# Loading q for two chunks at a time, and transposing q and k by the DMA from chunk 8 on, in a retention kernel fused with a feed-forward

## The chip, the cores and the metric

The kernel runs on one core of a Trainium2 chip. The core has five engines with instruction streams of their own: TensorE (PE; its weight loads are listed apart as PEld), VectorE (DVE), ScalarE (ACT), GpSimd (POOL) and SyncE (SP), which here issues the DMAs. The metric is the device time of one execution in microseconds, as the median of several runs. Profiles come from one execution with the hardware profiler on.

## The reference

Per batch and head a recurrent state is decayed and read at each token; the result, with the heads side by side, goes through a feed-forward with a product in the middle.

```python
batch, n_heads, seq, head_dim = (4, 8, 768, 64)
gamma = 1.0 - 2.0 ** (-5.0 - np.arange(H, dtype=np.float32))
for t in range(S):
    state = gamma[None, :, None, None] * state + np.einsum('bhd,bhe->bhde', k[:, :, t], v[:, :, t])
    y[:, :, t] = scale * np.einsum('bhd,bhde->bhe', q[:, :, t], state)
...
x = np.ascontiguousarray(attn_out.transpose(0, 2, 1, 3)).reshape(B * S, H * D)
a = x @ w1
b = x @ w2
h = a * b @ w3
return (h @ w_out).astype(np.float32)
```

All inputs and the output are float32; x is 3072 x 512, w1 and w2 are 512 x 1024, w3 is 1024 x 1024 and w_out 1024 x 512.

## The kernel before

The sequence is cut into chunks of 128 tokens, six for each of the four batches, 24 in all. Heads go in four pairs p, so that one pair fills 128 partitions. Work is done in float16 with float32 sums. The order of all instructions is written out by hand: each engine takes its own in the order of the Python code, and semaphores join them.

At the start w3 and w_out are multiplied into one matrix W3O (w3_transpose, w3_mm), while weights and the first chunks are loaded; chunks 0 and 1 and the feed-forward's first block are woven into this. From chunk 2 on, step(n) does one chunk:

- load_chunk(n+4) issues the loads of q, k and v of a later chunk on the SP queue (L61), each 128 tokens by 8 heads of 64 floats.
- casts(n+2) on GpSimd makes q16 and k16 (L214, L216) and the scaled v in vp (L220).
- transposes(n+1) on TensorE turns the four 128x128 blocks of k16 and the four of q16 through the identity into one PSUM tile psT (L234, L236). ScalarE copies k into kp (L239, L240): head 0 of a pair on the upper 64 partitions, head 1 on the lower, zeros elsewhere, so that one matmul works on one head. VectorE copies q into qT (L241).
- scores(n): eight matmuls of kp with qT (L252, psA), masked by VectorE into am (L255).
- kv(n): the chunk's contribution to the state (L273, psK); VectorE adds the old state (L281), GpSimd multiplies by the decay (L282). In a batch's last chunk kv does nothing.
- outputs(n): vp with am, and the old state with qT, summed in psY (L290, L291, L293); VectorE scales it into XT (L294), the transposed x.

Between these parts fill.pull puts in units of the feed-forward for blocks of 256 tokens: an a unit and a b unit (four matmuls each, L310; ScalarE copies a into pa, L320; VectorE multiplies into ht, L326), and o units (eight matmuls, L331; ScalarE scales into osb, L336; SP stores it, L338). fill is a queue; each pull takes a quarter of the units that the finished tokens allow in this step. What is left after the last step is run at the end.

XT is one tile for all tokens. The pools give q16 two buffers and k16 three; each chunk tensor loaded has six.

Of the kernel before, what the change touches and what calls it, by code (L numbers as in the profile page):

```python
# [9 lines left out]
FP = mybir.dt.float32  # L10
HP = mybir.dt.float16
AF = mybir.ActivationFunctionType
MULT = mybir.AluOpType.mult
# [5 lines left out]
def kernel(  # L19
# [15 lines left out]
    NCH = S // C  # L35
    NSTEP = B * NCH
    NTOK = B * S
    NP = H // 2
    DM = 512
    DFF = 1024  # L40
# [7 lines left out]
    xpool = ctx.enter_context(tc.tile_pool(name="xpool", bufs=1))  # L48
# [11 lines left out]
    def dma_in(dst, src):  # L60
        nc.sync.dma_start(dst, src)  # L61

    chunk_in = {}

    def load_chunk(n):
        if n >= NSTEP:
            return
        b, c = divmod(n, NCH)
        tiles = []
        for nm, src in (("q", q), ("k", k), ("v", v)):  # L70
# [51 lines left out]
    nc.gpsimd.iota(if_i[:, :], pattern=[[1, 128]], base=1, channel_multiplier=0)  # L122
    LGH = const.tile([128, H], FP, name="LGH")
    LGP = const.tile([128, NP], FP, name="LGP")
    for h in range(H):
# [5 lines left out]
    nc.gpsimd.memset(keep[:, :], 1.0)  # L131
    nc.gpsimd.affine_select(
        out=keep[:, :], in_=keep[:, :], compare_op=mybir.AluOpType.is_ge, fill=0.0,
        base=0, pattern=[[1, 128]], channel_multiplier=-1,
    )


# [16 lines left out]
        nc.vector.memset(GS[r : r + 64, p, r : r + 64], gam[h] ** C)  # L154
    zero(VP[2])

    XT = xpool.tile([128, NP, NTOK], HP, name="xt")

# [47 lines left out]
    q16s, k16s, qTs, ATs = {}, {}, {}, {}  # L206
    Tst = [None]

    def casts(n):
        if n >= NSTEP:  # L210
            return
        q32, k32, v32 = chunk_in.pop(n)
        q16 = att.tile([128, 512], HP, tag="q16", name="q16")
        nc.gpsimd.tensor_copy(q16[:, :], q32[:, :])  # L214
        k16 = att.tile([128, 512], HP, tag="k16", name="k16", bufs=3)
        nc.gpsimd.tensor_copy(k16[:, :], k32[:, :])  # L216
        vp = VP[n % 3]

        for r in range(2):
            nc.gpsimd.tensor_tensor(  # L220
                vp[:, :, r, r * 64 : r * 64 + 64],
                v32[:, :].rearrange("j (p s e) -> j p s e", s=2, e=64)[:, :, r, :],
                VS[:, :].rearrange("j (p s) -> j p s", s=2)[:, :, r].unsqueeze(2).broadcast_to((128, NP, 64)),
                MULT,
            )
        q16s[n], k16s[n] = q16, k16

    def transposes(n):
        if n >= NSTEP:
            return  # L230
        q16, k16 = q16s.pop(n), k16s[n]
        ps = ps_t.tile([128, 2, NP, 128], HP, tag="psT", name="psT")
        for p in range(NP):
            nc.tensor.transpose(ps[:, 1, p, :], k16[:, p * 128 : (p + 1) * 128], ident16[:, :])  # L234
        for p in range(NP):
            nc.tensor.transpose(ps[:, 0, p, :], q16[:, p * 128 : (p + 1) * 128], ident16[:, :])  # L236
        kp = KP[n % 2]
        qT = att.tile([128, NP, 128], HP, tag="qT", name="qT")
        nc.scalar.copy(kp[0:64, :, 0, :], ps[0:64, 1, :, :])  # L239
        nc.scalar.copy(kp[64:128, :, 1, :], ps[64:128, 1, :, :])  # L240
        nc.vector.tensor_copy(qT[:, :, :], ps[:, 0, :, :])  # L241
        qTs[n] = qT

    def scores(n):
        qT, kp = qTs[n], KP[n % 2]
        am = att.tile([128, NP, 2, 128], HP, tag="am", name="am")
        for half in range(2):
            ps = ps_at.tile([128, 2, 2, 128], FP, tag=f"psA{half}", name=f"psA{half}")
            for i in range(2):
                p = half * 2 + i  # L250
                for r in range(2):
                    nc.tensor.matmul(  # L252
                        ps[:, i, r, :], lhsT=kp[:, p, r, :], rhs=qT[:, p, :], start=True, stop=True
                    )
            nc.vector.tensor_tensor(  # L255
                am[:, half * 2 : half * 2 + 2, :, :].rearrange("j p s i -> j (p s) i"),
                ps[:, :, :, :].rearrange("j p s i -> j (p s) i"),
                keep[:, :].unsqueeze(1).broadcast_to((128, 4, 128)),
                MULT,
            )  # L260
        ATs[n] = am

    def kv(n):
        k16, vp = k16s.pop(n), VP[n % 3]
        c = n % NCH
        if c == NCH - 1:
            return None
        ps = ps_at.tile([128, NP, 128], FP, tag="psK", name="psK")
        for p in range(NP):

            rhs = vp[:, p, :, :].rearrange("j s e -> j (s e)")
            rhs = bass.AP(rhs.tensor, rhs.offset, [list(rhs.ap[0]), [192, 2], [1, 64]])
            nc.tensor.matmul(  # L273
                ps[:, p, :], lhsT=k16[:, p * 128 : (p + 1) * 128], rhs=rhs, start=True, stop=True
            )
        t16 = att.tile([128, NP, 128], HP, tag="t16", name="t16")
        if c == 0:
            nc.vector.tensor_tensor(t16[:, :, :], ps[:, :, :], GS[:, :, :], MULT)
        else:
            s32 = att.tile([128, NP, 128], FP, tag="s32", name="s32")  # L280
            nc.vector.tensor_tensor(s32[:, :, :], ps[:, :, :], Tst[0][:, :, :], ADD)  # L281
            nc.gpsimd.tensor_tensor(t16[:, :, :], s32[:, :, :], GS[:, :, :], MULT)  # L282
        return t16

    def outputs(n, t_new):
        am, qT, vp = ATs.pop(n), qTs.pop(n), VP[n % 3]
        c = n % NCH
        ps = ps_at.tile([128, NP, 128], FP, tag="psY", name="psY")
        for p in range(NP):
            nc.tensor.matmul(ps[:, p, :], lhsT=vp[:, p, 0, :], rhs=am[:, p, 0, :], start=True, stop=False)  # L290
            nc.tensor.matmul(ps[:, p, :], lhsT=vp[:, p, 1, :], rhs=am[:, p, 1, :], start=False, stop=(c == 0))  # L291
            if c > 0:
                nc.tensor.matmul(ps[:, p, :], lhsT=Tst[0][:, p, :], rhs=qT[:, p, :], start=False, stop=True)  # L293
        nc.vector.tensor_tensor(  # L294
            XT[:, :, n * C : (n + 1) * C], ps[:, :, :], YS[:, :, :], MULT
        )
        Tst[0] = t_new

# [3 lines left out]
    class Ffn:  # L302
# [4 lines left out]
        def mm(self, W, f):  # L307
            ps = ps_f.tile([128, TB], FP, tag="psF", name="psF")
            for d in range(4):
                nc.tensor.matmul(  # L310
                    ps[:, :], lhsT=W[d][:, f * 128 : (f + 1) * 128],
                    rhs=XT[:, d, self.tok0 : self.tok0 + TB],
                    start=(d == 0), stop=(d == 3),
                )
            return ps
# [62 lines left out]
    def step(n):  # L378

        ready = n * C  # L380
        share = fill.available(ready) / (2 - n % 2)
        casts(n + 2)
        transposes(n + 1)
        fill.pull(share * 0.25, ready)
        scores(n)
        fill.pull(share * 0.25, ready)
        t_new = kv(n)
        fill.pull(share * 0.25, ready)
        outputs(n, t_new)
        fill.pull(share * 0.25, ready)  # L390

    def cast_w(W, st, d, on_dve):
# [26 lines left out]
    w3_transpose(4)  # L419
    casts(0)  # L420
    w3_mm(3)
    transposes(0)
    cast_w3(5)
    w3_mm(4)
# [34 lines left out]
    def by_rows(W, ps, d):  # L459
        for f in range(8):  # L460
            nc.tensor.matmul(
                ps[f // 2][:, f % 2, :], lhsT=W[d][:, f * 128 : (f + 1) * 128],
                rhs=XT[:, d, 0:TB], start=(d == 0 and f % 2 == 0),
                stop=(d == 3 and f % 2 == 1),
            )

# [10 lines left out]
    for d in range(4):  # L477
        by_rows(W2, ps, d)
        if d == 1:
            transposes(2)  # L480
            casts(3)
    for i in range(4):
# [45 lines left out]
```

## Time and profile before

| | |
|---|---|
| median of 3 runs | 209.92 us (209.89 to 210.04) |
| profiled execution | 210.8 us |
| its span, first to last instruction | 209.0 us |
| granted TensorE clock | 1.000 |
| DMA: packets, bytes | 81239, 35.96 MB |
| of the packets, under 512 bytes | 75584 |

The span is what the profile shows; the profiled execution's own time is 1.8 us longer, and 0.9 us above the median. In the page's slices each digit is the busy share of a fortieth of the span in tenths. Groups give busy time in all, the mean of one in nanoseconds and the idle time before. Matmuls are pipelined, so the time of one in a group is longer than what it adds to a stream; the chain of work shows the latter. In rows of windows stand the stretch and its length, the busy time of PE, PEld, DVE, ACT and POOL with the number of instructions, the granted clock, the DMA share and GB/s.

### The profile page before, as it was taken

To read this page: it belongs to the slowest core of one execution; us is meant where nothing else is said; L and a number is where in the kernel's file an instruction comes from. 1 tells how busy PE (TensorE), PEld (TensorE's weight loads), DVE (VectorE), ACT (ScalarE), POOL (GpSimd) and SP (SyncE) were. 2 spreads that over 40 slices of the span, in tenths; PEclk is the share of its full clock that TensorE was granted. 3 is DMA by queue.
4 is the path that set the end of the run, shared out by engine and by line. 5 is a ranking of instruction groups with operands and counts; after the bars stand their busy time and mean duration, and the time that the engine had idled before them with its cause. 6 is when DMAs were issued, how large, how long until landed. Compare 5 with 4: busy or idle time off the path is not lost.

```text
span 209.0 us, 4850 instructions
## 1 busy us (share of the span) xinstructions
PE 197.2 (94%) x1848; PEld 148.3 (71%) x1848; DVE 118.6 (57%) x243; ACT 91.3 (44%) x187; POOL 78.5 (38%) x138
## 2 busy tenths in 40 slices
PE   6979699889999999999999999999999999999992
PEld 1435476666899778777877787787778877877750
DVE  4553479457777476448545854684367447753310
ACT  6463694343554425532544354335424542533331
POOL 4005302276895343663533336536331462010000
PEclk9999999999999999999999999999999999999999
DMA  6999999999999888459756865795578110111112
GB/s 231 390 359 211 305 391 413 216 221 207 232 252 207 185 168 188 109 117 195 162 116 129 201 157 111 139 201 139 115 153 200 57 49 4 50 50 53 50 50 102
DMA packets 81239, 35.96 MB, mean 172 GB/s; under 512 B 75584, under 2 KB 75584, under 8 KB 81216
## 3 DMA queue, kind: packets, MB, share of 16 engines
q1 hardware_dynamic: 81216, 35.66, 67.9%
q8 instruction: 14, 0.23, 0.5%
q14 instruction: 9, 0.07, 0.1%
HBM read 29.36 MB, written 6.29 MB: 171 GB/s over the span
## 4 chain that ended last, share of the span: by engine, by line
PE 76%; DMA 11%; SPq 6%; ACT 2%; DVE 2%; issue 1%; POOL 0%; ACTq 0%
PE psF L310 38%; PE psO L331 18%; DMA stg<-in_moe_w_dram 8%; SPq L61 6%; PE psA L252 4%; PE psW L199 2%; PE psT L234 2%; PE psT L236 2%; PE psY L290 2%; DMA k<-in_k_dram 2%; PE psY L291 2%; PE psY L293 2%; PE psK L273 2%; DVE am L255 1%; ACT kp L239 1%
## 5 line engine op out<-in xcount | busy, mean ns | idle before, releaser
L310 PE MATMUL psF<-xt,w 128*128 128x256 f16 x704 | 87.5, 272 | 0.2
L310 PEld LDWEIGHTS <-w 128*128 128x128 f16 x704 | 67.0, 97 | 9.6 <-issue 0.9
L320 ACT COPY pa<-psF 128x256 f32<-128x256 f32 x88 | 31.1, 373 | 36.3 <-PE psF L310 35.9
L331 PE MATMUL psO<-w3o,ht 128*128 128x512 f16 x192 | 45.0, 379 | 0.0
L282 POOL TENSOR_TENSOR t<-s,GS 128x512 f16<-128x512 f32 x16 | 20.3, 1270 | 58.3 <-DVE s L281 58.3
L241 DVE COPY qT<-psT 128x512 f16<-128x512 f16 x24 | 10.2, 425 | 55.7 <-ACT kp L240 55.7
L326 DVE TENSOR_TENSOR ht<-pa,psF 128x256 f16<-128x256 f32 x88 | 35.1, 416 | 10.6 <-ACT pa L320 6.1
L336 ACT ACTIVATE osb<-psO 128x512 f32<-128x512 f32 x24 | 14.3, 597 | 51.6 <-PE psO L331 51.6
L220 POOL TENSOR_TENSOR vp<-v,VS 128x256 f16<-128x256 f32 x48 | 28.5, 615 | 11.9 <-PE psY L291 6.9
L255 DVE TENSOR_TENSOR am<-psA,keep 128x512 f16<-128x512 f32 x48 | 30.8, 683 | 0.7 <-PE psA L252 0.7
L331 PEld LDWEIGHTS <-ht 128*128 128x128 f16 x192 | 17.9, 98 | 17.5
L214 POOL CAST q<-q 128x512 f16<-128x512 f32 x24 | 14.6, 610 | 23.2 <-DMA q<-in_q_dram 20.8
L216 POOL CAST k<-k 128x512 f16<-128x512 f32 x24 | 14.7, 614 | 10.5 <-PE psK L273 5.4
L294 DVE TENSOR_TENSOR xt<-psY,YS 128x512 f16<-128x512 f32 x24 | 16.6, 690 | 1.7 <-PE psY L293 0.5
L239 ACT COPY kp<-psT 64x512 f16<-64x512 f16 x24 | 13.7, 571 | 8.2 <-PE psT L236 8.2
L290 PE MATMUL psY<-am,vp 128*128 128x128 f16 x96 | 16.7, 219 | 0.2
L291 PE MATMUL psY<-am,vp 128*128 128x128 f16 x96 | 16.7, 219 | 0.0
L199 PE MATMUL psW<-wo,w3t 128*128 128x512 f16 x64 | 15.1, 379 | 0.0
L252 PE MATMUL psA<-qT,kp 128*128 128x128 f16 x192 | 14.6, 219 | 0.0
L293 PE MATMUL psY<-qT,t 128*128 128x128 f16 x80 | 14.5, 219 | 0.0
L240 ACT COPY kp<-psT 64x512 f16<-64x512 f16 x24 | 13.9, 581 | 0.4
L252 PEld LDWEIGHTS <-kp 128*128 128x128 f16 x192 | 12.6, 98 | 1.1 <-issue 0.3
(53 smaller groups left out, 173.0 us busy)
## 6 DMA issues: line engine op xcount, KB each, us to landing
stg<-in_moe_w_dram SPq DMA_DIRECT2D x16, 512.0 KB, 9.2
q<-in_q_dram SPq DMA_DIRECT2D x24, 256.0 KB, 3.9
k<-in_k_dram SPq DMA_DIRECT2D x24, 256.0 KB, 4.5
v<-in_v_dram SPq DMA_DIRECT2D x24, 256.0 KB, 5.1
out_dram<-osb SPq DMA_DIRECT2D x24, 256.0 KB, 2.2
stg<-in_moe_w_out_dram SPq DMA_DIRECT2D x4, 512.0 KB, 6.7
```

Of the source, the lines that this page charges most:

```text
L199: nc.tensor.matmul(ps[:, :], lhsT=t[:, g * 128 : (g + 1) * 128], rhs=WO[g // 2][:, g % 2, :], start=(g == 0), stop=(g == 7),)
L220: nc.gpsimd.tensor_tensor(vp[:, :, r, r * 64 : r * 64 + 64], v32[:, :].rearrange("j (p s e) -> j p s e", s=2, e=64)[:, :, r, :], VS[:, :]. ...
L252: nc.tensor.matmul(ps[:, i, r, :], lhsT=kp[:, p, r, :], rhs=qT[:, p, :], start=True, stop=True)
L255: nc.vector.tensor_tensor(am[:, half * 2 : half * 2 + 2, :, :].rearrange("j p s i -> j (p s) i"), ps[:, :, :, :].rearrange("j p s i -> j ( ...
L282: nc.gpsimd.tensor_tensor(t16[:, :, :], s32[:, :, :], GS[:, :, :], MULT)
L290: nc.tensor.matmul(ps[:, p, :], lhsT=vp[:, p, 0, :], rhs=am[:, p, 0, :], start=True, stop=False)
L291: nc.tensor.matmul(ps[:, p, :], lhsT=vp[:, p, 1, :], rhs=am[:, p, 1, :], start=False, stop=(c == 0))
L293: nc.tensor.matmul(ps[:, p, :], lhsT=Tst[0][:, p, :], rhs=qT[:, p, :], start=False, stop=True)
L310: nc.tensor.matmul(ps[:, :], lhsT=W[d][:, f * 128 : (f + 1) * 128], rhs=XT[:, d, self.tok0 : self.tok0 + TB], start=(d == 0), stop=(d == 3),)
L320: nc.scalar.copy(self.pa[f][:, :], ps[:, :])
L326: nc.vector.tensor_tensor(self.HT[:, f, :], self.pa.pop(f)[:, :], ps[:, :], MULT)
L331: nc.tensor.matmul(psO[:, :], lhsT=self.HT[:, f, tb * 128 : (tb + 1) * 128], rhs=W3O[f][:, :], start=(f == 0), stop=(f == 7),)
```

## The change

q is loaded once for two chunks (256 tokens) into q64: partition i holds the tokens 2i and 2i+1 of all heads, so that a run in memory has 128 floats in place of 64. q16 holds the even tokens in its first half and the odd ones in its second; one cast makes it for two chunks. In a chunk's queries the even tokens therefore stand ahead of the odd ones; the mask keep, the factors YS and the columns of psY follow this order, and the write into XT puts the tokens back, with a step of two elements. XT becomes one tile per 256 tokens, in a pool of four.

For chunks 0 to 7 TensorE transposes q for two chunks at once (q_transposes, eight transposes, one copy by VectorE for each chunk) and k for each chunk. From chunk 8 on (DT0) dma_transposes, called in step n for chunk n+2, issues a transposing DMA from SBUF to SBUF for k (into kT) and in even steps one for q of two chunks (into qTd). VectorE copies kT into kp; this part of transposes(n+1) now stands after outputs(n) and one pull, instead of ahead of scores(n). scores and outputs read their queries as two pieces of 64 columns from qTd.

```diff
+        if c % 2 == 0:
+
+            t = ld.tile([128, 2 * 512], FP, tag="q64", name="q64", bufs=3)
+            dma_in(
+                t[:, :].rearrange("p (h x) -> p h x", x=2 * D),
+                q[b, :, c * C : (c + 2) * C, :].rearrange("h (p t) d -> p h (t d)", t=2),
+            )
+            q_in[n // 2] = t
+        for nm, src in (("k", k), ("v", v)):
...
+        if n % 2 == 0:
+            q16 = att.tile([128, 1024], HP, tag="q16", name="q16")
+            nc.gpsimd.tensor_copy(
+                q16[:, :].rearrange("i (t h d) -> i h t d", t=2, d=D),
+                q_in.pop(n // 2)[:, :].rearrange("i (h t d) -> i h t d", t=2, d=D),
+            )
...
+    def q_transposes(m):
+
+        if m >= DT0 // 2:
+            return
+        q16 = q16s.pop(m)
...
+        for p in range(NP):
+            for t in range(2):
+                c0 = t * 512 + p * 128
+                nc.tensor.transpose(ps[:, p, t, :], q16[:, c0 : c0 + 128], ident16[:, :])
+        for c in range(2):
+            qT = att.tile([128, NP, 128], HP, tag="qT", name="qT", bufs=4)
+            nc.vector.tensor_copy(
+                qT[:, :, :].rearrange("p a (t i) -> p (a t) i", t=2),
+                ps[:, :, :, c * 64 : (c + 1) * 64].rearrange("p a t i -> p (a t) i"),
+            )
...
+    def dma_transposes(n):
+
+        if n < DT0 or n >= NSTEP:
+            return
+        kT = att.tile([128, NP, 128], HP, tag="kT", name="kT", bufs=2)
+        nc.sync.dma_start_transpose(kT[:, :, :], k16s[n][:, :])
+        kTs[n] = kT
+        if n % 2 == 0:
+            qT = att.tile([128, 2, NP, 128], HP, tag="qTd", name="qTd", bufs=2)
+            nc.sync.dma_start_transpose(
+                qT[:, :, :, :].rearrange("p t a i -> p (t a) i"), q16s.pop(n // 2)[:, :]
+            )
+            qTd[n // 2] = qT
...
+        if n >= DT0:
+            kT, kp = kTs.pop(n), KP[n % 2]
+            nc.vector.tensor_copy(kp[0:64, :, 0, :], kT[0:64, :, :])
+            nc.vector.tensor_copy(kp[64:128, :, 1, :], kT[64:128, :, :])
+            return
...
         casts(n + 2)
-        transposes(n + 1)
-        fill.pull(share * 0.25, ready)
+        if n + 1 < DT0:
+            transposes(n + 1)
+            fill.pull(share * 0.25, ready)
         scores(n)
         fill.pull(share * 0.25, ready)
         t_new = kv(n)
+        dma_transposes(n + 2)
+        if n % 2:
+            q_transposes((n + 1) // 2)
         fill.pull(share * 0.25, ready)
         outputs(n, t_new)
+        if n + 1 >= DT0:
+            fill.pull(share * 0.25, ready)
+            transposes(n + 1)
         fill.pull(share * 0.25, ready)
```

TensorE has 256 rows less in its program, a weight load and a matmul for each of 128 transposes. Two places show what moves. The first is VectorE in the middle of the program, from the last feed-forward product of a step to the masks of the next scores. Before:

```order
L326 TENSOR_TENSOR ht<-pa,psF 128x256
L294 TENSOR_TENSOR xt<-psY,YS 128x4x128
L241 COPY qT<-psT 128x512
L326 TENSOR_TENSOR ht<-pa,psF 128x256
L255 TENSOR_TENSOR am<-psA_1586,keep 128x512
```

and with the change, at the same place:

```order
L338 TENSOR_TENSOR s_1552<-psK,t_1434 128x512
L388 TENSOR_TENSOR ht<-pa,psF 128x256 x2
L355 TENSOR_TENSOR xt<-psY,YS 128x4x2x64
L388 TENSOR_TENSOR ht<-pa,psF 128x256
L290 COPY kp_158<-kT 64x4x128
L291 COPY kp_158<-kT 64x4x128
L312 TENSOR_TENSOR am<-psA_1629,keep 128x512
L312 TENSOR_TENSOR am<-psA_1635,keep 128x512
```

The copy of q has gone, and two copies of k stand behind one feed-forward product and straight ahead of the masks of scores, whose matmuls read kp.

The second is the SP queue in the same stretch. Before, three loads and one store per step:

```order
L338 DMA out_dram<-osb 128x512
L61 DMA q_1539<-in_q_dram 128x8x64
L61 DMA k_1541<-in_k_dram 128x8x64
L61 DMA v_1543<-in_v_dram 128x8x64
L338 DMA out_dram<-osb 128x512
```

and with the change, for two steps, the odd one ahead:

```order
L270 DMA_TRANSPOSE kT<-k_1624 128x4x128
L400 DMA out_dram<-osb 128x512
L62 DMA q_1723<-in_q_dram 128x8x128
L62 DMA k_1725<-in_k_dram 128x8x64
L62 DMA v_1727<-in_v_dram 128x8x64
L270 DMA_TRANSPOSE kT<-k_1731 128x4x128
L274 DMA_TRANSPOSE qTd<-q_1729 128x8x128
L400 DMA out_dram<-osb 128x512
L62 DMA k_1837<-in_k_dram 128x8x64
L62 DMA v_1839<-in_v_dram 128x8x64
```

The transposing DMAs stand in the one queue of loads and stores, behind the loads of a chunk four steps ahead and ahead of the next store; in every second step there is no load of q.

More of the change, by code (lines that the diff above doesn't have):

```diff
@@ L37 @@
     NTOK = B * S
+    DT0 = 8
     NP = H // 2
@@ L47 @@
     wstage = ctx.enter_context(tc.tile_pool(name="wstage", bufs=WST))
-    xpool = ctx.enter_context(tc.tile_pool(name="xpool", bufs=1))
+    xpool = ctx.enter_context(tc.tile_pool(name="xpool", bufs=4))
     ld = ctx.enter_context(tc.tile_pool(name="ld", bufs=6))
@@ L63 @@
     chunk_in = {}
+    q_in = {}
     def load_chunk(n):
@@ L69, in load_chunk @@
         tiles = []
-        for nm, src in (("q", q), ("k", k), ("v", v)):
+        if c % 2 == 0:
[6 more added lines that the diff above has]
+        for nm, src in (("k", k), ("v", v)):
             t = ld.tile([128, 512], FP, tag=nm + "32", name=nm + "32")
@@ L121 @@
     if_i = const.tile([128, 128], mybir.dt.int32, name="if_i")
-    nc.gpsimd.iota(if_i[:, :], pattern=[[1, 128]], base=1, channel_multiplier=0)
+    nc.gpsimd.iota(if_i[:, :], pattern=[[1, 2], [2, 64]], base=1, channel_multiplier=0)
     LGH = const.tile([128, H], FP, name="LGH")
@@ L133 @@
         out=keep[:, :], in_=keep[:, :], compare_op=mybir.AluOpType.is_ge, fill=0.0,
-        base=0, pattern=[[1, 128]], channel_multiplier=-1,
+        base=0, pattern=[[1, 2], [2, 64]], channel_multiplier=-1,
     )
@@ L155 @@
     zero(VP[2])
-    XT = xpool.tile([128, NP, NTOK], HP, name="xt")
+    XT = {}
     W1 = [wpool.tile([128, DFF], HP, name=f"w1_{i}") for i in range(4)]
@@ L203, in w3_mm @@
         cast_to(W3O[f][:, :], ps[:, :], f < 2)
-    q16s, k16s, qTs, ATs = {}, {}, {}, {}
+    q16s, k16s, qTs, ATs, kTs, qTd = {}, {}, {}, {}, {}, {}
     Tst = [None]
@@ L211, in casts @@
             return
-        q32, k32, v32 = chunk_in.pop(n)
-        q16 = att.tile([128, 512], HP, tag="q16", name="q16")
-        nc.gpsimd.tensor_copy(q16[:, :], q32[:, :])
+        k32, v32 = chunk_in.pop(n)
+        if n % 2 == 0:
[4 more added lines that the diff above has]
+            )
+            q16s[n // 2] = q16
         k16 = att.tile([128, 512], HP, tag="k16", name="k16", bufs=3)
@@ L225, in casts, with queries @@
             )
-        q16s[n], k16s[n] = q16, k16
+        k16s[n] = k16
+    def q_transposes(m):
+        if m >= DT0 // 2:
+            return
+        q16 = q16s.pop(m)
+        if m < 2:
+            ps = ps_at.tile([128, NP, 2, 128], HP, tag="psA0", name="psTq")
+        else:
+            ps = ps_t.tile([128, NP, 2, 128], HP, tag="psT", name="psTq")
+        for p in range(NP):
[8 more added lines that the diff above has]
+            )
+            qTs[2 * m + c] = qT
+    def dma_transposes(n):
[10 more added lines that the diff above has]
+            qTd[n // 2] = qT
+    def queries(n, p):
+        if n < DT0:
+            return qTs[n][:, p, :]
+        c = n % 2
+        return qTd[n // 2][:, :, p, c * 64 : (c + 1) * 64]
     def transposes(n):
@@ L230, in transposes @@
             return
-        q16, k16 = q16s.pop(n), k16s[n]
-        ps = ps_t.tile([128, 2, NP, 128], HP, tag="psT", name="psT")
+        if n >= DT0:
[3 more added lines that the diff above has]
+            return
+        k16 = k16s[n]
+        ps = ps_t.tile([128, NP, 128], HP, tag="psT", name="psT")
         for p in range(NP):
-            nc.tensor.transpose(ps[:, 1, p, :], k16[:, p * 128 : (p + 1) * 128], ident16[:, :])
-        for p in range(NP):
-            nc.tensor.transpose(ps[:, 0, p, :], q16[:, p * 128 : (p + 1) * 128], ident16[:, :])
+            nc.tensor.transpose(ps[:, p, :], k16[:, p * 128 : (p + 1) * 128], ident16[:, :])
         kp = KP[n % 2]
[L238 to L242, printed above, removed]
+        nc.scalar.copy(kp[0:64, :, 0, :], ps[0:64, :, :])
+        nc.scalar.copy(kp[64:128, :, 1, :], ps[64:128, :, :])
     def scores(n):
-        qT, kp = qTs[n], KP[n % 2]
+        kp = KP[n % 2]
         am = att.tile([128, NP, 2, 128], HP, tag="am", name="am")
@@ L252, in scores @@
                     nc.tensor.matmul(
-                        ps[:, i, r, :], lhsT=kp[:, p, r, :], rhs=qT[:, p, :], start=True, stop=True
+                        ps[:, i, r, :], lhsT=kp[:, p, r, :], rhs=queries(n, p), start=True, stop=True
                     )
@@ L285, in outputs @@
     def outputs(n, t_new):
-        am, qT, vp = ATs.pop(n), qTs.pop(n), VP[n % 3]
+        am, vp = ATs.pop(n), VP[n % 3]
         c = n % NCH
@@ L292, in outputs @@
             if c > 0:
-                nc.tensor.matmul(ps[:, p, :], lhsT=Tst[0][:, p, :], rhs=qT[:, p, :], start=False, stop=True)
+                nc.tensor.matmul(ps[:, p, :], lhsT=Tst[0][:, p, :], rhs=queries(n, p), start=False, stop=True)
+        if n % 2 == 0:
+            XT[n // 2] = xpool.tile([128, NP, 256], HP, tag="xt", name="xt")
+        order = "p a (t i) -> p a t i"
         nc.vector.tensor_tensor(
-            XT[:, :, n * C : (n + 1) * C], ps[:, :, :], YS[:, :, :], MULT
+            XT[n // 2][:, :, n % 2 * C : (n % 2 + 1) * C].rearrange("p a (i t) -> p a t i", t=2),
+            ps[:, :, :].rearrange(order, t=2), YS[:, :, :].rearrange(order, t=2), MULT,
         )
@@ L311, in mm @@
                     ps[:, :], lhsT=W[d][:, f * 128 : (f + 1) * 128],
-                    rhs=XT[:, d, self.tok0 : self.tok0 + TB],
+                    rhs=XT[self.tok0 // TB][:, d, :],
                     start=(d == 0), stop=(d == 3),
@@ L421 @@
     w3_mm(3)
+    q_transposes(0)
     transposes(0)
@@ L462, in by_rows @@
                 ps[f // 2][:, f % 2, :], lhsT=W[d][:, f * 128 : (f + 1) * 128],
-                rhs=XT[:, d, 0:TB], start=(d == 0 and f % 2 == 0),
+                rhs=XT[0][:, d, :], start=(d == 0 and f % 2 == 0),
                 stop=(d == 3 and f % 2 == 1),
@@ L479 @@
         if d == 1:
+            q_transposes(1)
             transposes(2)
```

## The prediction

> **What bounds the kernel now.** I read the page first: busy times, then the slices, then the chain that ended last.
>
> ```profile
> span 209.0 us, 4850 instructions
> PE 197.2 (94%) x1848; PEld 148.3 (71%) x1848; DVE 118.6 (57%) x243; ACT 91.3 (44%) x187; POOL 78.5 (38%) x138
> ...
> DMA  6999999999999888459756865795578110111112
> ...
> PE 76%; DMA 11%; SPq 6%; ACT 2%; DVE 2%; issue 1%; POOL 0%; ACTq 0%
> ```
>
> The reader is to see two stages. TensorE carries 76% of the chain; DMA and its queue carry 17%, and the DMA slices are full only up to the sixteenth. The chain in order of time shows where one stage ends and the other begins, so I read one whole step there (a step is one chunk of 128 tokens; this is step 14, counted by the pairs of psT rows):
>
> ```profile
> 54.04 1.03 PE psF L310 x8
> ...
> 120.60 0.22 PE psT L234 x4
> 120.82 0.22 PE psT L236 x4
> 121.05 1.31 PE psF L310 x12
> 122.36 0.45 PE psA L252 x8
> 122.80 1.40 PE psF L310 x12
> 124.21 0.22 PE psK L273 x4
> 124.43 0.89 PE psF L310 x8
> 125.99 1.73 PE psO L331 x8
> 127.71 0.22 PE psT L234 x4
> ...
> 184.40 1.31 PE psF L310 x12
> ```
>
> From 54.04 us on the chain is TensorE with one piece starting as the last ends. The step lasts 127.71 - 120.60 = 7.11 us and nothing waits in it. What leaves TensorE here leaves the time, as long as nothing else becomes late.
>
> **What the change takes from TensorE.** Eight transposes for each of the chunks 8 to 23: four of k (L234) and four of q (L236). In the chain they hold 121.05 - 120.60 = 0.45 us of a step, 56 ns each (the 219 ns of the page's group is mostly pipeline). 16 chunks x 8 x 0.0556 = **7.1 us**. The k and q transposes of chunks 0 to 7 stay on TensorE, eight a chunk on average as before, so they give nothing. A pair of steps goes from 14.2 to 13.3 us. ScalarE loses its two copies into kp (L239, L240) in these steps; it is off the path, so that is worth nothing.
>
> **What VectorE gets instead.** The copy of q from PSUM (L241) goes, and two copies kT to kp come, 64x512 in f16, from SBUF. They now stand after outputs and the first half of the fill that follows, and the next scores wait for them.
>
> ```profile
> L241 DVE COPY qT<-psT 128x512 f16<-128x512 f16 x24 | 10.2, 425 | 55.7 <-ACT kp L240 55.7
> L294 DVE TENSOR_TENSOR xt<-psY,YS 128x512 f16<-128x512 f32 x24 | 16.6, 690 | 1.7 <-PE psY L293 0.5
> ...
> 57.99 1.04 PE L310 MATMUL psF<-xt,w 128*128 128x256 f16 x8
> 58.39 0.68 DVE L294 TENSOR_TENSOR xt<-psY,YS 128x512 f16<-128x512 f32 x1
> 59.14 0.42 DVE L326 TENSOR_TENSOR ht<-pa,psF 128x256 f16<-128x256 f32 x1
> ```
>
> The last three rows, from the timeline, are an outputs followed by two feed-forward units, which is the order that all later steps will have. Counted from the first psF matmul (57.99), VectorE is free after ht at 59.56, or 1.57 us. TensorE does the two units (0.87) and an o unit (1.73 in the chain) before it comes to the scores, at 2.60. So 1.0 us is there for two copies. The nearest row, L241, is 0.425 us for the same 512 f16 elements: 0.85 us, done at 2.42, **no stall, with 0.2 us to spare**. At zero they would also be free; at the 0.69 us of L294 they would end at 2.95 and scores would wait 0.35 us a step, 5.6 us over sixteen. I take nothing, and keep 5.6 as the upper end. xt's write with every second element, the two-piece reads of q in scores and outputs, and q's cast in one instruction per pair keep their element counts; I give them nothing.
>
> **What the DMA gets.** Per pair of chunks two transposes of 128x512 and one of 128x1024, in f16: 512 KB read and written in SBUF. No row of this trace shows a transposing DMA. First the room:
>
> ```profile
> 78.14:163.06 84.92, 84.87 (x851) 67.83 (x849) 50.39 (x106) 36.41 (x84) 37.66 (x57) 1.00 0.69 150
> 30.00:35.00 5.00, 5.00 (x44) 3.08 (x42) 5.00 (x8) 2.82 (x5) 1.27 (x1) 1.00 1.03 419
> 40.00:45.00 5.00, 3.29 (x33) 2.51 (x30) 2.03 (x4) 1.34 (x3) 3.08 (x6) 1.00 1.00 206
> 184.40:209.00 24.60, 20.39 (x156) 14.17 (x154) 6.93 (x15) 7.73 (x18) 0.00 (x0) 1.00 0.17 65
> q<-in_q_dram SPq DMA_DIRECT2D x24, 256.0 KB, 3.9
> SPq L338 <- ACT osb L336: 80.4, 19, 6.7
> ```
>
> In the windows the last two columns are the DMA share and GB/s. The first row is twelve steps: 0.69 of 84.92 us, 9.8 us of DMA per pair. The other windows price bytes: the weights' rows of 4 KB went at 419 GB/s, and the loads of q, k and v, in runs of 256 bytes, at 206, which is 1.27 us for 256 KB; the stores at the end took 0.17 x 24.6 = 4.2 us for 65 x 24.6 = 1.6 MB, six of them, so 1.4 us for two. In the change q is read in runs of 512 bytes. Time per run on 16 engines is 156 ns for 4 KB and 20 ns for 256 bytes; a line between them gives 29 ns for 512 bytes, so 1.86 us for a pair's q instead of 2.54: 0.7 us less. Room for transposes is then 13.3 - 9.8 + 0.7 = 4.2 us per pair. Their bounds: 1.3 us at 419 GB/s; 2.5 us at 206; and 11.7 us if each of the three had the queue to itself for the 3.9 us that a q load needs to land. I take 2.5, the row nearest in kind, since a transpose also moves runs of 128 f16 elements, 256 bytes. **It fits, so I cost it at nothing.**
>
> Two pages of the Trainium skill disagree on this price, and no run here shows either. "VectorE: DVE Perf Modes", section "The three transpose paths", gives 1309 ns for one 128x128 block through the DMA against 390 on TensorE: sixteen blocks one after another would be an estimated 20.9 us per pair, and the change would lose. "Advanced Engine Details and Errata", section "X-Bar Transpose (TRN2)", expects 350 to 400 GB/s, an estimated 1.3 to 1.5 us. The 390 ns of the first page is not what a transpose costs in this stream, where the chain shows 56, so its 1309 may not hold in a stream either.
>
> Latency is covered: the transposes of chunk n+2 are issued in step n, as soon as its casts are done, and the copies of kT are at the end of step n+1, the first use of qTd at the start of step n+2. That is a step or more, 6.7 us, against 3.9 to land. The SP queue has the time as well: it waited 80.4 us in all for osb, 19 times, so 4.2 us a step. Behind a transpose that waits for its cast stand only the next osb store and loads that are four chunks ahead.
>
> **The start.** Until 52 us the DMA queue sets the pace, through the loads of chunks 0 to 4:
>
> ```profile
> 48.49 0.61 POOL L216 CAST k<-k 128x512 f16<-128x512 f32 x1 [0.98 <-DMA k<-in_k_dram]
> 49.69 1.19 POOL L220 TENSOR_TENSOR vp<-v,VS 128x256 f16<-128x256 f32 x2 [0.59 <-DMA v<-in_v_dram]
> 50.84 1.26 POOL L282 TENSOR_TENSOR t<-s,GS 128x512 f16<-128x512 f32 x1
> ...
> 52.16 0.22 PE L290 MATMUL psY<-am,vp 128*128 128x128 f16 x1
> ```
>
> v of chunk 4 lands, GpSimd scales it, makes the state t, and outputs of step 3 begin at 52.16. Up to that v the queue carried five q loads, 6.4 us; it will carry three pairs, 5.6 us by the line above: 0.8 us earlier. Bounds: at 1.25 us a pair 2.6 us earlier, at 2.54 us a pair 1.3 us later (chunk 5's q then comes ahead of chunk 4's v for nothing). Some of it will be caught by the next wait in this short chain, so I take **0.6 us**.
>
> **The sum.** The profiled execution took 210.8 us, 1.8 of it outside its span of 209.0. 209.0 - 7.1 - 0.6 = 201.3 us of span, 203.1 with what lies around it. The median of the runs is 209.92, 0.9 below the profiled one; so **202.2 us**.
>
> **The rivals.**
> *A, the scores wait at every step (chance 0.12).* The mechanism is VectorE's two copies, or a kT that lands late. For it: only 0.2 us of cover remain by the nearest row, and VectorE comes to the copies late, behind xt and ht. Against it: L241 reads PSUM and writes all 128 partitions, the new copies read SBUF and write half of them. At 0.2 to 0.35 us a step it takes back 3.2 to 5.6 us: 205.4 to 207.8.
> *B, the DMA queue becomes the bound (0.15), slower.* The first transposes are issued in step 6, near 66 us, when the queue is still full. From there it must do seven pairs of loads at 9.8 - 0.7 - 1.4 (the stores) = 7.7 us, so 54, eight pairs of stores, 11, and eight pairs of transposes at T each; and after chunk 23's keys come the 24.6 us from 184.40 to the end. 66 + 65 + 8T + 25 = 209 gives T = 6.6 us: the queue starts to show above 4.2 us per pair, and the kernel is slower than before above 6.6. At the 11.7 us of three serial landings the span is 250. For it: the DMA is already 0.69 busy, and the operation is unknown. Against it: 2.5 us by the row nearest in kind. With the figure of the Trainium skill's "VectorE: DVE Perf Modes", 20.9 us for T, the same sum would give an estimated 323.
> *C, the TensorE time does not go away (0.03).* If the transposes were filled into gaps, their removal would give nothing, and the time is 209.9, or what the start gives. The chain speaks against it: no gap is next to them.
> The forecast keeps 0.70.
>
> **How the numbers follow.** Faster by over 0.2% (about what a measurement of this kernel can tell from no change): forecast and A, 0.82. Within: 0.03. Slower: B, 0.15. The range goes from the start's full gain, 209.92 - 7.1 - 2.6 = 200.2, to A's upper end, 207.8; B and C are left out with 0.18.
>
> **What would show it.** Right: a step near 122 us lasts 6.66 us in the chain, from psA to psA, with nothing between psO and psA; DMA share stays below 1 after 75 us; psF's first row comes near 53.4 instead of 54.04. Wrong: TensorE idle before L309 (the scores) ended by VectorE's kp (A) or by the DMA of kT or qTd (B); a transposing DMA that takes over 4 us from issue to landing with the queue full (B); the first psF later than 54.04 (the start's other sign).

## The result, and the profile after

The changed kernel took 201.41 us, the median of 4 runs (200.68 to 201.65), beside 209.98 for the kernel before on the same chip: a ratio of 0.957 (95% interval 0.953 to 0.962). The prediction was 202.2 us, 200.2 to 207.8. The total came out; two terms behind it, both put at nothing, did not, and their errors offset each other in part. In the runs below, executions over 1.5% above their kernel's fastest are left out of medians and ratios: three of e7_double_dma, the profiled one among them, two of e8_dt4_kp_scalar, and one each of e10 and e11.

The page of the changed kernel:

```profile
span 199.7 us, 4580 instructions
PE 187.6 (94%) x1720; PEld 140.3 (70%) x1720; DVE 131.8 (66%) x259; ACT 76.2 (38%) x155; POOL 77.4 (39%) x126
...
DMA  6999999999799998997999989979899732111103
...
PE 73%; DMA 12%; SPq 8%; DVE 3%; POOL 1%; ACT 1%; issue 1%; DVEq 0%; POOLq 0%
```

TensorE still carries the chain. New are the DMA slices, at seven tenths or more until the thirty-second in place of the sixteenth, and VectorE has 3% in place of 2%. The chain in order of time, at the start of the steps, around two steps, and where the leftover feed-forward begins after the last step:

```profile
53.31 1.03 PE psF L372 x8
...
94.05 0.89 PE psF L372 x8
...
95.36 0.72 DVE kp L290
96.10 1.02 DVE kp L291
97.18 0.56 PE psA L309 x7
...
109.97 0.45 PE psA L309 x8
110.41 1.31 PE psF L372 x12
111.72 0.22 PE psK L330 x4
111.95 1.31 PE psF L372 x12
...
116.53 0.49 PE psA L309 x8
...
182.32 3.49 PE psF L372 x32
```

The step from 109.97 to 116.53 is 6.56 us, against 7.11 before. That is 0.55 less, where eight transposes are 0.45. Against that stands the place near 97 us, where scores waited for VectorE's second copy of kT; it occurs again near 136.8.

Three sections can be told apart: the start, up to the first psF row; the steps, from there to the row of 32 psF matmuls; and the end. For the kernel before the rows are 54.04, quoted above, and this one:

```profile
190.92 3.49 PE psF L310 x32
```

| kernel | first psF | x32 | steps |
|---|---|---|---|
| before | 54.04 | 190.92 | 136.88 |
| changed | 53.31 | 182.32 | 129.01 |

The start gained 0.73 us and the steps 7.87. So the steps gave 0.75 us more than 128 transposes at 0.0556, although a new wait had come in. Something else had left, and the experiments look for it.

### The profile page after: what moved, and what is told of

Same layout as the page of the kernel before. It is cut to its first block, busy times and chain, and to the rows that moved or that the text cites. A ratio compares the mean times of both kernels' runs of the same rounds, so it can differ in the third digit from the quotient of the medians.

```text
span 199.7 us, 4580 instructions
## 1 busy us (share of the span) xinstructions
PE 187.6 (94%) x1720; PEld 140.3 (70%) x1720; DVE 131.8 (66%) x259; ACT 76.2 (38%) x155; POOL 77.4 (39%) x126
## 4 chain that ended last, share of the span: by engine, by line
PE 73%; DMA 12%; SPq 8%; DVE 3%; POOL 1%; ACT 1%; issue 1%; DVEq 0%; POOLq 0%
PE psF L372 39%; PE psO L393 17%; DMA stg<-in_moe_w_dram 9%; SPq L62 8%; PE psA L309 5%; DMA v<-in_v_dram 3%; PE psW L210 3%; PE psY L348 2%; PE psY L347 2%; PE psY L350 2%; PE psK L330 2%; DVE kp L291 1%; PE psW L199 1%; DVE kp L290 1%; POOL t L339 1%
## 5 line engine op out<-in xcount | busy, mean ns | idle before, releaser
L382 ACT COPY pa<-psF 128x256 f32<-128x256 f32 x88 | 32.6, 372 | 55.4 <-PE psF L372 55.3
L388 DVE TENSOR_TENSOR ht<-pa,psF 128x256 f16<-128x256 f32 x88 | 36.6, 417 | 22.1 <-PE psF L372 13.4
L393 PEld LDWEIGHTS <-ht 128*128 128x128 f16 x192 | 18.7, 98 | 17.9
L226 POOL CAST q<-q 128x1024 f16<-128x1024 f32 x12 | 12.6, 1047 | 23.3 <-DMA q<-in_q_dram 23.3
L355 DVE TENSOR_TENSOR xt<-psY,YS 128x512 f16<-128x512 f32 x24 | 17.6, 733 | 2.7 <-PE psY L350 2.7
L338 DVE TENSOR_TENSOR s<-psK,t 128x512 f32<-128x512 f32 x16 | 11.0, 690 | 3.8 <-PE psK L330 1.9
L309 PE MATMUL psA<-qTd,kp 128*128 128x128 f16 x128 | 10.4, 220 | 0.9 <-DVE kp L291 0.9
L210 PEld LDWEIGHTS <-w3t 128*128 128x128 f16 x64 | 6.0, 98 | 5.9
L350 PE MATMUL psY<-qTd,t 128*128 128x128 f16 x56 | 10.1, 219 | 0.0
L183 ACT CAST w3h<-stg 128x1024 f16<-128x1024 f32 x8 | 8.3, 1044 | 3.8 <-DMA stg<-in_moe_w_dram 3.8
```

The lines of the kernel that those rows point to most:

```text
L210: nc.tensor.matmul(ps[:, :], lhsT=t[:, g * 128 : (g + 1) * 128], rhs=WO[g // 2][:, g % 2, :], start=(g == 0), stop=(g == 7),)
L309: nc.tensor.matmul(ps[:, i, r, :], lhsT=kp[:, p, r, :], rhs=queries(n, p), start=True, stop=True)
L355: nc.vector.tensor_tensor(XT[n // 2][:, :, n % 2 * C : (n % 2 + 1) * C].rearrange("p a (i t) -> p a t i", t=2), ps[:, :, :].rearrange(orde ...
L382: nc.scalar.copy(self.pa[f][:, :], ps[:, :])
L388: nc.vector.tensor_tensor(self.HT[:, f, :], self.pa.pop(f)[:, :], ps[:, :], MULT)
L393: nc.tensor.matmul(psO[:, :], lhsT=self.HT[:, f, tb * 128 : (tb + 1) * 128], rhs=W3O[f][:, :], start=(f == 0), stop=(f == 7),)
```

## The experiments

Times in this section are medians of their runs, ratios are to the kernel before on the same chip. The column "steps" of the summary is read from the two rows of the chain, as above.

### First set: what each half is worth

**e1_tensor_all**: q loaded for two chunks as in the change, all transposes on TensorE, k's at the start of the step.

```diff
-    DT0 = 8
+    DT0 = 24
```

> DT0 is 24 in place of 8: no DMA transposes and no kT copies; q still loaded and cast for two chunks, all 24 chunks transposed by TensorE. It keeps the start of the change and gives back the TensorE time. Theory 1 (start 0.7 us, 128 transposes 7.1 us, and 1.7 us more because ScalarE's copies into kp held the feed-forward's PSUM tiles back in every step): 209.3 us, since the copies into kp are back in their old place. Theory 2 (the held-back tiles came from VectorE's copy of q, which waited behind ScalarE's copies): that copy no longer stands in every step, so 207.6 to 208 us, with psF x12 after psA at 1.31 us in the chain. Rival: the extra 1.7 us belongs to the loads and tiles that this kernel keeps, not to the transposes: also 207.6, but with psF x12 at 1.41.

Measured: 212.74 us, 1.011 (1.008 to 1.015), slower than before and than each expectation. The extra gain does not belong to the loads and tiles kept here. In its chain ScalarE's osb, two copies into kp and pa stand ahead of 16 psF rows of 12 matmuls, each of 1.47 us, where all but one of the changed kernel's 30 rows are at 1.31. The next run has the same row of ScalarE.

**e2_q_by_dma**: only q through the DMA; k's transposes, and ScalarE's copies into kp, at the start of every step as before.

```diff
-        kT = att.tile([128, NP, 128], HP, tag="kT", name="kT", bufs=2)
-        nc.sync.dma_start_transpose(kT[:, :, :], k16s[n][:, :])
-        kTs[n] = kT
...
-        if n + 1 < DT0:
-            transposes(n + 1)
-            fill.pull(share * 0.25, ready)
+        transposes(n + 1)
+        fill.pull(share * 0.25, ready)
```

> Only q is transposed by the DMA from chunk 8 on; k stays on TensorE and ScalarE, at the old place in the step. 64 transposes less, 3.6 us. Theory 1 (ScalarE's copies alone hold the feed-forward back): the stall of 0.1 us a step stays, 209.98 - 0.7 - 3.6 = 205.7 us. Theory 2 (it needs VectorE's copy of q behind them): it goes, 204.1 us. If the DMA transposes of k are what loads the DMA queue, DMA share in the steps falls from 1.0 to about 0.85.

Measured: 209.99 us, 0.998 (0.996 to 1.000). Both forecasts fell: 64 transposes had gone from TensorE, and the time stayed. The DMA share between 72 and 164 us was 0.78, beside 0.63 in e1_tensor_all and 1.01 in the changed kernel, so k's transposes are over half of the added load. Its timeline shows who set the pace; a row has start, length, engine, line and operation:

```profile
112.79 0.39 PE L288 MATMUL psT<-ident,k 128*128 128x128 f16 x4
112.99 0.60 ACT L390 ACTIVATE osb<-psO 128x512 f32<-128x512 f32 x1 [2.25 <-PE psO L385]
113.02 1.47 PE L364 MATMUL psF<-xt,w 128*128 128x256 f16 x12
113.49 0.57 ACT L290 COPY kp<-psT 64x512 f16<-64x512 f16 x1
114.06 0.58 ACT L291 COPY kp<-psT 64x512 f16<-64x512 f16 x1
114.33 0.61 PE L301 MATMUL psA<-qTd,kp 128*128 128x128 f16 x8
114.67 0.65 ACT L374 COPY pa<-psF 128x256 f32<-128x256 f32 x2
115.09 1.47 PE L364 MATMUL psF<-xt,w 128*128 128x256 f16 x12 [0.16 <-ACT pa L374]
```

ScalarE goes from osb through two copies into kp to pa, back to back from 112.99. pa frees the first of the three PSUM tiles of the feed-forward, and TensorE needs it for its fourth unit, the second psF row. TensorE now comes 0.16 us too early, and the first matmul after a wait adds its full 0.27 us in place of 0.11, which makes the row 1.47 us in place of 1.31. From the end of psO (112.97) to the fourth unit 2.12 us pass, and it is ScalarE's row that fills them, not TensorE's work.

The same stretch was in the kernel before; its rows:

```profile
113.52 0.60 ACT L336 ACTIVATE osb<-psO 128x512 f32<-128x512 f32 x1 [2.25 <-PE psO L331]
114.02 0.57 ACT L239 COPY kp<-psT 64x512 f16<-64x512 f16 x1
114.59 0.58 ACT L240 COPY kp<-psT 64x512 f16<-64x512 f16 x1
115.20 0.65 ACT L320 COPY pa<-psF 128x256 f32<-128x256 f32 x2
115.21 0.43 DVE L241 COPY qT<-psT 128x512 f16<-128x512 f16 x1 [2.69 <-ACT kp L240]
115.60 0.42 DVE L326 TENSOR_TENSOR ht<-pa,psF 128x256 f16<-128x256 f32 x1
```

There eight transposes filled the time, and the chain showed TensorE throughout. But ht, which frees the second tile, came after pa and after VectorE's copy of q; VectorE had been idle for 2.69 us, until ScalarE's second copy into kp ended. The sign was in the rows of the prediction: both psF rows have 12 matmuls, one took 1.31 us, the one after psA 1.40.

**e4_before_kp_split**: the kernel before with one line changed.

```diff
-        nc.scalar.copy(kp[64:128, :, 1, :], ps[64:128, 1, :, :])
+        nc.vector.tensor_copy(kp[64:128, :, 1, :], ps[64:128, 1, :, :])
```

> The kernel before with one edit: VectorE makes the second copy into kp, ahead of its copy of q, so that ScalarE and VectorE are both free 0.1 to 0.6 us earlier for pa and ht. If the 0.1 us a step that the change gained beyond its transposes is that delay, psF x12 after psA falls from 1.41 to 1.31 us in the chain and the time to about 208.4 us. Rival: the 1.41 has another cause (a bank or a weight load): 210.0 us, 1.41 stays.

Measured: 208.02 us, 0.989 (0.986 to 0.992); all 36 psF rows of 12 in its chain are at 1.31. The kernel before had this wait, and it came from ScalarE's copies in a row.

**e3_kp_on_scalar**: the change, with ScalarE making the copies of kT in the new place.

```diff
-            nc.vector.tensor_copy(kp[0:64, :, 0, :], kT[0:64, :, :])
-            nc.vector.tensor_copy(kp[64:128, :, 1, :], kT[64:128, :, :])
+            nc.scalar.copy(kp[0:64, :, 0, :], kT[0:64, :, :])
+            nc.scalar.copy(kp[64:128, :, 1, :], kT[64:128, :, :])
```

> As the changed kernel, but ScalarE makes the two copies of kT into kp, at the same place in the step. If the two stalls ahead of scores (0.5 us each near 97 and 136 us) and the longer first scores come from VectorE's copies, which take 0.3 to 1.0 us each: 0.9 to 1.2 us less than the changed kernel, 200.3 us, and L309 never waits for kp. Rival: ScalarE's copies take 0.58 us each and delay pa and osb, which holds back the feed-forward again: 201.4 or up to 203 us, with psF x12 above 1.31 us.

Measured: 199.64 us, 0.948 (0.945 to 0.951). TensorE is busy for the whole stretch from 72 to 164 us; its row of the windows, then that of the changed kernel (behind the stretch and its length stand PE, PEld, DVE, ACT, POOL, clock, DMA share and GB/s):

```profile
72.00:164.00 92.00, 92.00 (x893) 73.59 (x891) 58.59 (x112) 46.69 (x100) 43.90 (x60) 1.00 0.98 195
```

```profile
72.00:164.00 92.00, 91.06 (x877) 71.87 (x876) 70.36 (x138) 29.04 (x70) 44.42 (x59) 1.00 1.01 191
```

Here ScalarE's two copies run under the o unit, ahead of osb, and delay nothing, though two copies of this size closed the step before.

### Second set: ScalarE's place, and the queue

**e5_scalar_load_back**: the change, with two idle ScalarE copies put where the copies into kp had been.

```diff
+        elif n + 1 < NSTEP:
+            idle = att.tile([128, 512], HP, tag="idle", name="idle")
+            nc.scalar.copy(idle[0:64, :], k16s[n][0:64, :])
+            nc.scalar.copy(idle[64:128, :], k16s[n][64:128, :])
```

> The changed kernel with two added copies on ScalarE, of 64x512 each into a tile that nothing reads, at the start of each step from 7 on: the place and size of the copies into kp in the kernel before. TensorE, VectorE and DMA have nothing added. Theory 3, formed on the last runs: the step before was closed by ScalarE, osb then two copies into kp then pa, which frees the PSUM tile that the fourth feed-forward unit needs; the change gained by emptying that stretch as much as by its transposes. Then TensorE waits 0.15 to 0.3 us in each of 16 steps at psF behind psK: 203.8 to 206.2 us. Rival: ScalarE is idle over half of the time and the copies are hidden: 201.4 us.

Measured: 209.26 us, 0.992 (0.989 to 0.995). Two copies on an engine that is idle for more than half of the time take back most of the gain: 0.035 of the 0.043 in the ratio, and 7.4 of the 7.9 us in the steps. The sum of the expectation was too small. From the chain of its waiting stretch:

```profile
106.10 0.03 ACT osb L398
106.12 0.60 issue
106.72 0.28 ACT idle L450
107.00 0.34 issue
107.35 0.62 ACT idle L451
107.97 0.03 issue
107.99 0.38 ACT pa L382
108.37 0.04 issue
108.41 1.47 PE psF L372 x12
```

From 106.08 to the fourth unit at 108.41 pass 2.33 us, where scores, three units and psK need 1.98; and psF then takes 1.47 in place of 1.31, as in e2. That is 0.5 us a step, some 8 us.

**e6_tensor_late**: all transposes on TensorE, but k's, with ScalarE's copies, in the change's late place; q's in odd steps.

```diff
-    DT0 = 8
+    DT0 = 24
+    LATE = 8
...
-        if n + 1 < DT0:
+        if n + 1 < LATE:
             transposes(n + 1)
...
-        if n + 1 >= DT0:
+        if n + 1 >= LATE:
             fill.pull(share * 0.25, ready)
             transposes(n + 1)
```

> All transposes on TensorE as in e1_tensor_all, but from chunk 8 on k's transposes and copies into kp stand where the change has its copies of kT: after outputs and one pull, ahead of the o unit. No DMA transposes. Theory 3: ScalarE then copies into kp under the o unit's 1.73 us, ahead of osb, and nothing waits: the changed kernel plus 7.1 us of transposes less about 0.9 us of its stalls at kp, 207.6 us, 5 us less than e1_tensor_all and 2 less than before. Rival: TensorE's k transposes cost the same wherever they stand: 212.7 us.

Measured: 206.96 us, 0.981 (0.977 to 0.984), 3% below e1_tensor_all with the same instructions in another order. No DMA transposes are needed for this part.

**e7_double_dma**: the change with every transposing DMA issued twice, the second into a tile that nothing reads.

```diff
+        kT2 = att.tile([128, NP, 128], HP, tag="kT2", name="kT2", bufs=2)
+        nc.sync.dma_start_transpose(kT2[:, :, :], k16s[n][:, :])
```

(and the same for q).

> The changed kernel with every transposing DMA issued twice, the second into a tile that nothing reads. The queue of the prediction's rival B: with T of 4.2 us per pair as the DMA share now says (1.01 of 13.2 us less the 9.1 for loads and stores), 8.4 us twice, the sum 66 + 65 + 8 x 8.4 + 25 gives a span of 223, so about 225 us. Rival: the share of busy time counts waiting, the queue has room, and transposes are issued early enough: within 1 us of 201.4.

Measured: 213.71 us, 1.010 (1.005 to 1.015): slower than before, but less so than the sum. The waits of its profile (us in total, times, longest):

```profile
PE psA L316 <- DMA qTd<-q: 9.8, 5, 3.3
PEld L316 <- DVE kp L298: 8.4, 6, 3.8
...
DVE kp L297 <- DMA kT<-k: 5.7, 4, 3.1
```

and its queue, then those of the changed kernel and of e1_tensor_all, which has no transposing DMA (packets, MB, share of 16 engines' span):

```profile
q1 hardware_dynamic: 103040, 44.05, 94.2%
```

```profile
q1 hardware_dynamic: 85888, 39.86, 86.2%
```

```profile
q1 hardware_dynamic: 68736, 35.66, 64.4%
```

The second copy added 0.942 x 213.2 - 0.862 x 199.7 = 28.7 us of queue time, 3.6 per pair of chunks, and 17152 packets for 4.19 MB, 244 bytes each. The first copy added as many packets and 172.1 - 0.644 x 211.3 = 36.0 us, 4.5 per pair. With T = 2 x 3.6 the prediction's sum for rival B gives 66 + 65 + 58 + 25 = 214, with T = 3.6 + 4.5 it gives 221; the executions that count had spans of 209.8 to 212.2, the profiled one 213.2. So the sum is too long, by some 2 us at the least. Whether the transfers or their issue on the SP queue held the kernel back was not told apart.

**e8_dt4_kp_scalar**: e3_kp_on_scalar with DT0 = 4.

> DMA transposes from chunk 4 on (DT0 4), and the copies of kT on ScalarE as in e3_kp_on_scalar. If TensorE stays the bound: 32 transposes less, 1.8 us under e3's 199.6, 197.8 us. Rival: from step 2 to 6 the DMA queue is full with loads, and the transposes of chunks 4 to 7 push back the loads that the step waits for: 200 us or more, with TensorE idle before L309 between 45 and 70 us.

Measured: 207.47 us, 0.982 (0.977 to 0.987). The rival held, for chunk 4 alone, whose scores waited for both of its transposes behind the loads:

```profile
ACT kp L290 <- DMA kT<-k: 6.5, 1, 6.5
PE psA L309 <- DMA qTd<-q: 5.9, 1, 5.9
```

### Third set: side by side, and what order alone does

**e9_changed_again** is the changed kernel without an edit.

> The changed kernel itself, beside the next three on the same chip: 0.957 of the kernel before.

Measured: 201.73 us, 0.960 (0.957 to 0.963).

**e10_kp_on_scalar_again** is e3_kp_on_scalar.

> e3_kp_on_scalar beside the changed kernel: 0.948 of before, so about 0.991 of the changed kernel. If the two differ by less than 0.3% here, the gain of ScalarE's copies is not shown.

Measured: 200.03 us, 0.951 (0.947 to 0.954). The intervals of the two lie apart; ScalarE's copies are worth 0.9%, and this kernel is the fastest of the study.

**e11_dt6_kp_scalar** is e3_kp_on_scalar with DT0 = 6.

> DMA transposes from chunk 6 on, ScalarE copying kT. If the queue has room from step 4 on: 16 transposes less than e3, 0.9 us, 0.944 of before. Rival, after e8_dt4_kp_scalar: the loads still fill the queue at step 4, near 53 us, and scores(6) waits for kT or qTd: 0.955 or more.

Measured: 200.88 us, 0.958 (0.954 to 0.963). The rival again, smaller: in the chain a DMA into kT from 58.61 to 63.14, and the wait of PE for qTd 1.9 us, once.

**e12_before_late**: the kernel before, with all of transposes(n+1) in the late place from chunk 8 on.

```diff
-        transposes(n + 1)
-        fill.pull(share * 0.25, ready)
+        if n + 1 < 8:
+            transposes(n + 1)
+            fill.pull(share * 0.25, ready)
...
         outputs(n, t_new)
+        if n + 1 >= 8:
+            fill.pull(share * 0.25, ready)
+            transposes(n + 1)
```

> The kernel before with one edit: from chunk 8 on the eight transposes and their copies stand where the change has its copies of kT, behind outputs and one pull. Same loads, same TensorE work, no DMA transposes. Theory 3 (the step was closed by ScalarE's osb, kp, kp, pa and its place, 0.1 us a step): 1.3 to 2 us less than before, 0.991 to 0.994. Rival: e6_tensor_late gained by its q loads for two chunks: 1.000.

Measured: 211.43 us, 1.004 (1.002 to 1.006). Neither: in this order it was 0.4% slower. Its timeline in one step:

```profile
105.21 0.58 ACT L239 COPY kp<-psT 64x512 f16<-64x512 f16 x1 [0.51 <-PE psT L236]
105.82 0.58 ACT L240 COPY kp<-psT 64x512 f16<-64x512 f16 x1
106.43 0.42 DVE L241 COPY qT<-psT 128x512 f16<-128x512 f16 x1 [1.17 <-ACT kp L240]
...
106.91 0.61 PE L252 MATMUL psA<-qT,kp 128*128 128x128 f16 x8
```

k and q lie in one PSUM tile, and VectorE's copy of q again waits for ScalarE's. Three copies in a row end just as scores want qT, and psA takes 0.61 us of its chain in place of 0.45. In e6_tensor_late q is transposed elsewhere in the step: there the late place gained, with q's copy in the row it did not.

### The summary

| kernel | ratio | steps, us |
|---|---|---|
| before | 1 | 136.88 |
| changed, e9 | 0.957, 0.960 | 129.01, 128.98 |
| e1_tensor_all | 1.011 | 139.71 |
| e2_q_by_dma | 0.998 | 136.88 |
| e3, e10 | 0.948, 0.951 | 127.41, 127.41 |
| e4_before_kp_split | 0.989 | 134.94 |
| e5_scalar_load_back | 0.992 | 136.43 |
| e6_tensor_late | 0.981 | 134.55 |
| e12_before_late | 1.004 | 137.36 |

e3, with no wait in the steps, has 127.41 us; with 128 transposes more that is 127.41 + 7.12 = 134.53, and e6, which has just these, has 134.55. The sections hold equal work: 1382 TensorE matmuls, transposes among them, before and in e1, e4, e6 and e12, and 128 less, 1254, in the changed kernel, e3 and e5. In e3 and e6 TensorE is busy for the whole section. So TensorE's own work is known in both forms, and the rest of each row is waiting: 2.35 us before, 0.4 left in e4, 1.60 in the changed kernel.

## Why the prediction was right or wrong

**The transposes, 7.1 us: right in size, for a reason that was half of it.** e6 less e3 is 7.14 us. But the prediction took it that nothing waits in a step, so that whatever leaves TensorE leaves the time. e2_q_by_dma shows the opposite: with half of the transposes gone the steps had the same 136.88 us, because ScalarE's osb, kp, kp, pa set the length of that stretch. The transposes came out as time because k's copies left ScalarE's stretch in the same change.

**ScalarE's copies, "worth nothing": wrong.** The steps before held 2.35 us of waiting; e4, which moves one of the copies to VectorE, takes back 1.94 of it, and e5 shows that two such copies in that place undo most of the change. The prediction called ScalarE off the path, as the chain has it in these steps; the stretch between osb and pa was not read.

**VectorE's copies, no stall: wrong, and mis-sized.** They cost 129.01 - 127.41 = 1.60 us. The forecast was 0.425 us for each copy. Their groups (times, then ns as shortest, median and longest), and the slowest pair in the timeline, with GpSimd's rows beside it:

```profile
L290 DVE COPY kp<-kT x16: 277/528/709, 75.6 to 174.7; 64x512 f16<-64x512 f16 x16
L291 DVE COPY kp<-kT x16: 291/292/1015, 76.1 to 175.0; 64x512 f16<-64x512 f16 x16
```

```profile
94.73 1.20 POOL L236 TENSOR_TENSOR vp<-v,VS 128x256 f16<-128x256 f32 x2
95.36 0.71 DVE L290 COPY kp<-kT 64x512 f16<-64x512 f16 x1
95.86 1.11 POOL L226 CAST q<-q 128x1024 f16<-128x1024 f32 x1
96.10 1.01 DVE L291 COPY kp<-kT 64x512 f16<-64x512 f16 x1
```

The copy takes 0.28 us alone and up to 1.0 beside GpSimd. This is rival A's mechanism, VectorE's copies ahead of scores, at half of the lower size that it was given (3.2 to 5.6 us). The 1.0 us of room in the prediction was about right. In nine steps the two copies took 0.6 to 1.0 us together and psA kept its 0.45 us. In five they took 1.1 to 1.2 us and psA 0.49 to 0.59. Near 97 and 137 us they took 1.7 us, because the second met the cast of q for two chunks, which the change itself had made one instruction of 1.1 us; against e3 each of these two cost some 0.6 us, most of the 1.60.

**The DMA, nothing: right, but close, and at too low a price.** Of the three lengths weighed, 2.5 us per pair was taken and 3.6 to 4.5 measured, in packets of about 256 bytes as assumed; the room was put at 4.2. The DMA share rose from 0.69 to 1.01 in the steps, against the forecast that it would stay below 1, and still no scores waited for a transpose: they were issued early enough. A share of 1.01 was not the end of the queue, since e7 had 1.11 between 72 and 164 us. Rival B's break-even of 6.6 us lies between the price in the change and the 7.2 or more of e7, which was 1% slower than before.

**The signs.** Of the signs for right, the step came (6.56 us) and the first psF row (53.31); the DMA share did not stay below 1. Of the signs for wrong, A's showed in two steps, as said. B's showed too: kT landed 2.4 to 6.1 us after its issue, a median of 5.0, where over 4 was to mean that the queue was the bound. It was not; the time from issue to landing includes the loads ahead in the queue, and scores came later still.

**The start, 0.6 us:** 0.73 between the two profiles. Over the kernels of the study that keep the change's start the first psF row lay between 52.42 and 54.06 us, without e7 and e8, in the three with the old one between 54.04 and 55.32. All but one of the nine lie below the lowest of the three, so the sign is borne out; the size is of the order of its scatter.

**The sum.** 7.1 + 0.6 were forecast; the compute chain gained 190.92 - 182.32 = 8.60, which is 0.73 + 7.12 + 2.35 - 1.60. The two terms that were missed offset each other but for 0.75. What remains of the 9.3 us between the spans, 0.7, lies behind the start of the last osb (204.85 to 209.0 before, 196.25 to 199.7 now) and was not followed up. The span was forecast at 201.3 and came to 199.7. That the median, 201.41, lay within 0.8 of its forecast is in part luck: the prediction took off 0.9 us because the profiled execution before stood that far above its median, and here the two agree (201.44).

## What to carry to other kernels

An engine at 44%, absent from the chain in the steps, can still set the length of a stretch when its operations stand in a row in front of the one that frees a buffer. Compare equal rows of the chain: 12 matmuls at 1.31 us in one place and 1.40 in another are a wait that the chain calls work. Before work is taken from the engine that bounds, follow every buffer that it takes in that stretch to the engine that frees it; here half of the removal gave nothing, and the order of the same instructions was worth 3%.

## What the runs showed of the hardware that was not expected

- A VectorE copy of 64x512 f16 within SBUF took 0.28 to 0.29 us in the 15 of the changed kernel's 32 copies during which GpSimd was idle, and 0.52 to 1.01 us in the 17 that began while it worked. In the rows above L290 ends 0.14 us after GpSimd's operation (95.93), and L291 0.14 us after the cast (96.97). The Trainium skill, "SBUF — State Buffer", section "Who interferes with whom", says that VectorE's faster modes and GpSimd take one shared port pair in turn, each for a whole instruction; these ends agree with that. No run here tried the mode itself.
- A DMA transpose was slower to move and to issue than a plain DMA. 512 KB in 3.6 to 4.5 us of queue time are 116 to 146 GB/s, beside 206 for the loads in 256-byte runs. On the SP queue kT took 1.23 to 2.94 us and qTd, twice as large, 1.25 to 1.31, where a plain load or store in the same stretch took 0.33 to 1.55. The Trainium skill, "Advanced Engine Details and Errata", section "X-Bar Transpose (TRN2)", expects 350 to 400 GB/s; in this kernel, beside the loads, the measurement was well below.
- kT, 128 KB, landed a median of 5.0 us after its issue, and qTd, 256 KB, 3.2 us. This goes with the place in the queue and not with the size: in e2_q_by_dma, where qTd stands directly behind the loads, as kT does here, it took a median of 2.68 us on the SP queue and landed after 5.0.
